# RWKV-6 attention with a SiLU block: level-5 scores in array quarters that serve both batch rows at once, instead of in array eighths

## The chip, the cores and the metric

The kernel runs on one core of one Trainium2 chip. The metric is the device time of a launch in microseconds (us). TensorE (PE) multiplies matrices into PSUM; VectorE (DVE), ScalarE (ACT) and GpSimd (POOL) do elementwise work; SyncE (SP) issues most of the DMA transfers. PEld names TensorE's weight loads, which overlap its matmuls.

## The reference, cut to what matters

First comes a recurrent attention over 768 tokens, for 4 batch rows and 8 heads of 48 channels; then a two-layer network over all 3072 tokens.

```python
for t in range(S):                      # S = 768, state: (B, H, 48, 48)
    cur = einsum('bhd,bhe->bhde', u * k[t], v[t])
    y[t] = einsum('bhd,bhde->bhe', r[t], state + cur)
    state = w[t][..., None] * state + einsum('bhd,bhe->bhde', k[t], v[t])
x = y.transpose(0, 2, 1, 3).reshape(B * S, H * D)     # 3072 x 384
h = x @ w_in                                          # 384 x 2048
out = (h * (1 / (1 + exp(-h)))) @ w_out               # 2048 x 384
```

The decay w multiplies the state per channel, so the weight of key s in the output of token t is the product of all decays between them. Everything is float32.

## The kernel before, in words

**Units.** The tokens are cut into 6 pieces of L = 128. Two batch rows (NB = 2) are worked on together, so there are 12 units, numbered 0 to 11, of 128 tokens by two batch rows. The 8 heads form NP = 4 pairs; the two heads of a pair (index `e`) lie on partitions 0 to 47 and 64 to 111. A row `q` of the tiles `tr` (queries) and `score` is a batch row and a pair, 8 in all.

**Levels.** Inside a unit, the score of query t and key s contains the decays between them. The kernel builds these products by halving. At level l the 128 tokens are cut into blocks of c = 2^l. Queries in an odd block meet the keys of the even block just before it; queries (`tr`) and keys (`tk`) have by then been multiplied with the decays up to the border between the two blocks. Level 6 has one pair of blocks of 64 tokens for a batch row, level 5 has two pairs of blocks of 32. Keys of the second batch row are kept in reversed order of time. That way the even blocks of both batch rows fit side by side in one row of 128 keys, `tk[i][rows, X[l % 2] + p, :]`: where one batch row has no keys to offer, the other has. `corner(l, x)` says which batch row and which query block the x-th stretch of c keys belongs to.

**Scores.** `score_products` (L688) computes one level of a unit on TensorE. In units 1 to 11 it doesn't use the whole array at once, but parts of it: `rows` picks one head of the pair, which is one half of the array's rows, and the stretch of keys picks a part of its columns. In quarters, 64 keys are the stationary matrix (48 x 64) and the moving matrix holds 64 queries. For levels 1 to 4 these are 32 queries of each of the two batch rows, so half of each result belongs to a key of one batch row and a query of the other, and nobody reads it. Level 6 has one batch row for each quarter. Level 5, before the change, is in eighths: 32 keys by 32 queries, one batch row each, four stretches for a pair and head.

**Readers.** In most units (2 to 11) `burst` computes two levels together, 3 with 4 and 5 with 6, into the PSUM tiles `p_sc` and `p_m` (`p_o` in unit 2). `keep_level` copies levels 5 and 6 into `score` with ScalarE (L801), block by block. Unit 1 instead copies under a mask (L722). Unit 0 has another form at L712 for levels 1 to 5, and so has level 4 of unit 2. After the burst, `grow_queries` (L627, DVE) multiplies the queries for the next step in place, and `y_state`, `y_values`, `update` use the scores.

**Order of work.** The order on each engine is written out by hand. From unit 3 on, the attention of unit i is interleaved with the network of units i - 1 and i - 2: `up` (L1001, the first layer, with the SiLU at L1010 on ScalarE), `sums` (L1049, DVE sums of activations for a seven-product scheme of the second layer) and `quarter` (L1067, the second layer, with DVE additions at L1076). `mix` lists the attention's groups, and the loop at L1166 puts network steps between them. `bonus_write` (L604) and `block_write` (L577) put the u-term on the diagonal of `score`. POOL multiplies the keys (`grow_keys`, L645) ahead of each burst. In the first 90 us, the weights are also brought into another form piece by piece (`head_weight`, `tail_weight`, `join_weight`, `add_weight`, L223 to L255).

Of the kernel before, what the change touches and what calls it, by code (L numbers as in the profile page):

```python
# [38 lines left out]
def kernel(  # L39
# [11 lines left out]
    nc = tc.nc  # L51
# [10 lines left out]
    X = 0, NP + Q  # L62
# [275 lines left out]
    for l in range(NL):  # L338
        c, ni = 1 << l, L >> (l + 1)
# [18 lines left out]
    tw, tr, tk, diag, kq, xt = {}, {}, {}, {}, {}, {}  # L358
# [320 lines left out]
    def dims_of(have, start, *dims):  # L679
        return bass.AP(tensor=have.tensor, offset=have.offset + start, ap=[have.ap[0], *dims])  # L680

    def corner(l, x):

        return x % 2, x if x % 2 == 0 else (L >> l) - 1 - x
# [3 lines left out]
    def score_products(i, l, queries, sc):  # L688
        c, ni = 1 << l, L >> (l + 1)
        if (i > 0 or l == NL - 1) and (i, l) != (NTOK, FIRST + 1):  # L690
            for p in range(NP):
                for x in range(4 if c == 32 else 2):
                    for e in range(2):
                        rows = slice(PD * e, PD * e + D)
                        if c >= 32:
                            b, first = corner(l, x)
                            q = (p, 2 * NP - 1 - p)[b]
                            to, have = sc[e][x * c:(x + 1) * c, q, first // 2 * c:(first // 2 + 1) * c], queries[rows, q, (first + 1) * c:(first + 2) * c]
                        else:
                            apart = 2 * (NP - p) - 1  # L700
                            to = dims_of(sc[e][x * 64:(x + 1) * 64, p, :], 32 * x, [apart * L // 2 + 32 - 64 * x, 2], [1, 32])
                            have = dims_of(queries[rows, p, :], 64 * x + c, [apart * L + 64 - 128 * x, 2], [2 * c, 32 // c], [1, c])
                        m = 32 if c == 32 else 64
                        nc.tensor.matmul(to, lhsT=tk[i][rows, X[l % 2] + p, x * m:(x + 1) * m], rhs=have, start=True, stop=True)  # L704
            return

        for p in range(NP):
            for e in range(2):
                rows = slice(PD * e, PD * e + D)

                apart, r_p, s_p = 2 * (NP - p) - 1, queries[rows, p, :], sc[e][:, p, :]
                nc.tensor.matmul(bass.AP(tensor=s_p.tensor, offset=s_p.offset,  # L712
                                         ap=[s_p.ap[0], [apart * L // 2, 2], [1, L // 2]]),
                                 lhsT=tk[i][rows, X[l % 2] + p, :],
                                 rhs=bass.AP(tensor=r_p.tensor, offset=r_p.offset + c,
                                             ap=[r_p.ap[0], [apart * L, 2], [2 * c, ni], [1, c]]),
                                 start=True, stop=True)
# [7 lines left out]
    def scores(i, l, *between):  # L725
        c, ni = 1 << l, L >> (l + 1)

        odd = i == 0 and l % 2 == 1
        sc = [ps.tile([128, Q, L // 2], F32, name="p_h", bufs=2) if odd else bank("p_sc", Q, L // 2) for e in range(2)]
        score_products(i, l, tr[i], sc)  # L730
        if i < NTOK and l + 2 < NL:
            odd_keys(i, l + 1)
# [53 lines left out]
    def burst(i, l):  # L786

        made[i, l] = [bank("p_sc", Q, L // 2) for e in range(2)]
        made[i, l + 1] = [second[0].tile([128, Q, L // 2], F32, name="p_o", bufs=2) if i == NTOK else bank("p_m", Q, L // 2) for e in range(2)]
        score_products(i, l, before.pop((i, l)), made[i, l])  # L790
        score_products(i, l + 1, tr[i], made[i, l + 1])
# [417 lines left out]
```

## Time and profile before

| | |
|---|---|
| median of 3 runs | 600.91 us (600.6, 600.91, 602.53) |
| the profiled execution's own time | 601.18 us |
| its span | 599.4 us |
| busy: PE, PEld | 590.6 us (99%), 529.7 us (88%) |
| busy: DVE, ACT, POOL | 417.5, 232.8, 361.3 us |
| DMA | 53.45 MB, 89 GB/s in the mean |
| matmul records at L704, the line concerned | 1312 into `p_sc`, 608 into `p_m`, 32 into `p_o` |

The span is the time from the first to the last instruction that the profiler recorded; the profiled execution's own time is 1.78 us longer, which lies around the span. A line of the profile names the engine, the source line, the operation and what it writes from what. `x` counts records; a float32 matmul of the program appears as two. Some matmul records can be missing. In square brackets stands how long the engine had been idle before the instruction, and which engine and line released it; "issue" means that it waited for nothing that the profile shows.

### The profile page before, as it was taken

Reading aid. Unit: us, or ns where it says so; the run is one execution under the profiler, and the core shown is the slowest. Engines: PE = TensorE matmul, PEld = TensorE weight load, DVE = VectorE, ACT = ScalarE, POOL = GpSimd, SP = SyncE. Lnnn points to the kernel's source line nnn. Section 1 sums busy time; section 2 is a strip of 40 time slices with the busy share of each in tenths; the row PEclk is TensorE's granted clock in tenths of the full one; section 3 lists DMA queues with packets and bytes.
Section 4 is the critical chain, followed back from the end, with each engine's and each line's share of the span. In section 5 each row is a group of like instructions: output and inputs, shape, how many; then the busy total and the mean of one; then the engine's idle time right before and its main releaser. Section 6 shows DMA issues by size and latency. Waiting matters only on the chain.

```text
span 599.4 us, 15465 instructions
## 1 busy us (share of the span) xinstructions
PE 590.6 (99%) x6142; PEld 529.7 (88%) x6142; DVE 417.5 (70%) x709; ACT 232.8 (39%) x516; POOL 361.3 (60%) x414
## 2 busy tenths in 40 slices
PE   8999999999999999999999999999999999999997
PEld 7787876799899899899899889889889889889997
DVE  7879788798696695696696696687588587542041
ACT  6788884431530530540350351361351251250110
POOL 6998778357678568278578478577567567500000
PEclk9999999999999999999999999999999999999999
DMA  9966794342542543642643643643543531101000
GB/s 225 306 143 176 165 277 49 54 80 48 129 61 62 108 68 54 134 63 52 137 63 54 134 61 53 135 61 53 112 77 52 121 57 27 36 2 28 27 1 26
DMA packets 203080, 53.45 MB, mean 89 GB/s; under 512 B 186752, under 2 KB 194816, under 8 KB 203008
## 3 DMA queue, kind: packets, MB, share of 16 engines
q1 hardware_dynamic: 201424, 51.88, 42.3%
q8 instruction: 48, 0.79, 0.6%
q10 hardware_dynamic: 1584, 0.59, 0.5%
q14 instruction: 24, 0.20, 0.1%
HBM read 43.21 MB, written 5.24 MB: 81 GB/s over the span
## 4 chain that ended last, share of the span: by engine, by line
PE 74%; DVE 9%; POOL 4%; DMA 4%; ACT 3%; issue 3%; SPq 3%; DVEq 0%; POOLq 0%; ACTq 0%
PE p_h L1001 31%; PE p_o L1067 31%; PE p_m L1023 3%; PE p_sc L704 2%; PE p_m L865 2%; DVE temps L1049 2%; SPq L123 1%; PE p_m L844 1%; PE p_m L704 1%; DVE score L722 1%; POOL w_in_sb L255 1%; DMA tokens_w<-in_w_dram 1%; POOL tk L645 1%; DVE p_w L242 1%; DMA raw<-in_r_dram 1%
## 5 line engine op out<-in xcount | busy, mean ns | idle before, releaser
L1001 PE MATMUL p_h<-xt,w_in_sb 128*128 128x256 f32 x1152 | 259.5, 382 | 0.8 <-POOL tk L669 0.7
L1001 PEld LDWEIGHTS p_h<-xt,w_in_sb 128*128 128x128 f32 x1152 | 215.6, 190 | 32.1 <-POOL tk L669 0.9
L1010 ACT ACTIVATE gt<-p_h 128x512 f32<-128x512 f32 x90 | 53.5, 596 | 175.4 <-PE p_h L1001 175.1
L645 POOL TENSOR_TENSOR tk<-tk,tw 128x256 f32<-128x256 f32 x128 | 94.6, 759 | 32.9 <-issue 20.8
L1067 PE MATMUL p_o<-own,temps 128*128 128x192 f32 x528 | 88.7, 327 | 0.7 <-DVE temps L1076 0.7
L1067 PEld LDWEIGHTS p_o<-own,temps 128*128 128x128 f32 x528 | 86.0, 190 | 1.6 <-DVE temps L1076 1.6
L507 POOL TENSOR_TENSOR ruk<-tokens_rk 128x768 f32<-128x768 f32 (+1 forms) x32 | 50.6, 1594 | 60.8 <-DMA tokens_rk<-in_k_dram 36.9
L1067 PE MATMUL p_o<-w_out_sb,gt 128*128 128x192 f32 x508 | 86.6, 327 | 0.0
L1067 PEld LDWEIGHTS p_o<-w_out_sb,gt 128*128 128x128 f32 x508 | 83.3, 190 | 1.0 <-DVE partial L1076 0.4
L1049 DVE TENSOR_TENSOR temps<-gt 128x256 f32<-128x256 f32 x84 | 54.9, 653 | 25.5 <-ACT gt L1010 25.3
L627 DVE TENSOR_TENSOR tr<-tr,tw 128x512 f32<-128x512 f32 x61 | 54.8, 899 | 18.3 <-PE p_m L704 14.6
L422 POOL TENSOR_TENSOR tw<-tw 128x256 f32<-128x256 f32 (+6 forms) x83 | 41.0, 494 | 35.8 <-DVE tw L374 31.9
L615 ACT COPY tk<-tk 128x256 f32<-128x256 f32 x52 | 21.0, 403 | 105.2 <-POOL tk L645 77.6
L1049 DVE TENSOR_TENSOR temps<-temps,gt 128x256 f32<-128x256 f32 x43 | 32.6, 759 | 1.5
L722 DVE COPY_PREDICATED score<-mask,p_sc 128x512 f32<-128x512 int8 x42 | 31.2, 799 | 3.5 <-PE p_sc L704 3.3
L1067 PE MATMUL p_o<-w_out_sb,temps 128*128 128x192 f32 x176 | 30.4, 326 | 0.0
L541 DVE TENSOR_REDUCE block_sums<-ruk 128x4 f32<-128x192 f32 (+1 forms) x48 | 24.2, 546 | 7.1 <-POOL ruk L507 7.1
L1067 PEld LDWEIGHTS p_o<-w_out_sb,temps 128*128 128x128 f32 x176 | 28.9, 190 | 0.0
L1076 DVE TENSOR_TENSOR partial<-p_o,partial 128x192 f32<-128x192 f32 x33 | 11.7, 354 | 24.6 <-PE p_o L1067 24.6
L1076 DVE TENSOR_TENSOR temps<-p_o,partial 128x192 f32<-128x192 f32 x22 | 7.9, 358 | 29.8 <-PE p_o L1067 23.5
L870 ACT COPY yt<-p_m 48x512 f32<-48x512 f32 x40 | 23.2, 580 | 13.8 <-PE p_m L865 13.1
L704 PEld LDWEIGHTS p_sc<-tr,tk 48*32 48x32 f32 (+1 forms) x1312 | 18.2, 119 | 11.1 <-issue 8.1
(188 smaller groups left out, 821.9 us busy)
## 6 DMA issues: line engine op xcount, KB each, us to landing
w_out_sb<-in_moe_w_in_dram SPq DMA_DIRECT2D x6, 768.0 KB, 7.5
w_out_sb<-in_moe_w_out_dram SPq DMA_DIRECT2D x4, 768.0 KB, 5.6
own<-in_moe_w_out_dram SPq DMA_DIRECT2D x4, 768.0 KB, 6.4
tokens_rk<-in_r_dram SPq DMA_DIRECT2D x8, 384.0 KB, 4.5
tokens_rk<-in_k_dram SPq DMA_DIRECT2D x8, 384.0 KB, 5.5
tokens_w<-in_w_dram SPq DMA_DIRECT2D x8, 384.0 KB, 6.6
xt<-yt SPq DMA_DIRECT2D x60, 48.0 KB, 2.0
raw<-in_w_dram SPq DMA_DIRECT2D x80, 32.0 KB, 2.0
```

What stands on the lines that cost most here:

```text
L422: engine.tensor_tensor(out=up, in0=t[:, :, 0::2], in1=t[:, :, 1::2], op=ALU.mult)
L507: mul = lambda out, one, two: nc.gpsimd.tensor_tensor(out=out, in0=one, in1=two, op=ALU.mult)
L541: add = lambda out, have: nc.vector.tensor_reduce(out=out, in_=have, axis=mybir.AxisListType.X, op=ALU.add)
L627: nc.vector.tensor_tensor(out=odd, in0=odd, in1=tw[i][l][:, :, 0::2][:, :, :, None].to_broadcast([128, Q, L >> (l + 1), c]), op=ALU.mult)
L645: nc.gpsimd.tensor_tensor(out=out, in0=have, in1=odd_products(i, l, b, *blocks), op=ALU.mult)
L704: nc.tensor.matmul(to, lhsT=tk[i][rows, X[l % 2] + p, x * m:(x + 1) * m], rhs=have, start=True, stop=True)
L722: nc.vector.copy_predicated(out=dst, mask=masks[l][:, :, None].to_broadcast([128, NB, NP, ni, c]), data=sc[e].rearrange("p (b q) (i c) -> ...
L870: nc.scalar.copy(out=yt[i][PD * e:PD * e + D, x::2, :, :], in_=p_yt[i, e][PD * x:PD * x + D].rearrange("p (q b) t -> p q b t", b=NB))
L1001: nc.tensor.matmul(p_h[:, a, :], lhsT=w_in_sb[:, c, f * 128:(f + 1) * 128], rhs=xt[i][:, c, :], start=(c == 0), stop=(c == KC - 1))
L1010: nc.scalar.activation(out=gt[i, m], in_=p_h, func=AF.Silu)
L1049: nc.vector.tensor_tensor(out=out, in0=one, in1=two, op=op)
L1067: nc.tensor.matmul(p, lhsT=left(f), rhs=right[:, f, :], start=(f == 0), stop=(f == FH - 1))
```

## The change

In `score_products`, level 5 (c = 32) no longer has its own branch. It takes the form of levels 1 to 4: two stretches of 64 keys instead of four of 32, and for each a moving matrix of 64 queries, 32 from each of the two batch rows. The special form with `corner` stays for level 6 (c = 64) alone. Level 5 of a unit is then 16 matmuls of 48 x 64 by 64, where it was 32 of 48 x 32 by 32. The results that are needed land at the same places of PSUM, and every reader is unchanged; as much again of the tile, which level 5 left unwritten, now gets products that nobody reads.

```diff
         if (i > 0 or l == NL - 1) and (i, l) != (NTOK, FIRST + 1):
             for p in range(NP):
-                for x in range(4 if c == 32 else 2):
+                for x in range(2):
                     for e in range(2):
                         rows = slice(PD * e, PD * e + D)
-                        if c >= 32:
+                        if c == 64:
                             b, first = corner(l, x)
                             q = (p, 2 * NP - 1 - p)[b]
                             to, have = sc[e][x * c:(x + 1) * c, q, first // 2 * c:(first // 2 + 1) * c], queries[rows, q, (first + 1) * c:(first + 2) * c]
                         else:
                             apart = 2 * (NP - p) - 1
                             to = dims_of(sc[e][x * 64:(x + 1) * 64, p, :], 32 * x, [apart * L // 2 + 32 - 64 * x, 2], [1, 32])
                             have = dims_of(queries[rows, p, :], 64 * x + c, [apart * L + 64 - 128 * x, 2], [2 * c, 32 // c], [1, c])
-                        m = 32 if c == 32 else 64
-                        nc.tensor.matmul(to, lhsT=tk[i][rows, X[l % 2] + p, x * m:(x + 1) * m], rhs=have, start=True, stop=True)
+                        nc.tensor.matmul(to, lhsT=tk[i][rows, X[l % 2] + p, x * 64:(x + 1) * 64], rhs=have, start=True, stop=True)
```

## The prediction

> **What bounds the kernel now.** I read the page's busy times first, then busy time by stage, then TensorE's own waits, then single bursts of level 5.
>
> ```profile
> PE 590.6 (99%) x6142; PEld 529.7 (88%) x6142; DVE 417.5 (70%) x709; ACT 232.8 (39%) x516; POOL 361.3 (60%) x414
> ```
>
> TensorE (PE) sets the time, but 99% is a mean. By stage (columns: span, then busy time of PE, weight loads, DVE, ACT, POOL):
>
> ```profile
> 88.90:180.40 91.50, 91.03 (x1040) 76.67 (x1040) 76.40 (x115) 35.23 (x84) 57.72 (x63) 1.00 0.44 72
> 180.40:273.10 92.70, 92.49 (x993) 84.72 (x993) 68.80 (x113) 30.67 (x76) 61.95 (x70) 1.00 0.44 80
> 273.10:557.20 284.10, 284.10 (x2945) 262.17 (x2946) 189.88 (x330) 89.82 (x223) 169.15 (x191) 1.00 0.37 69
> ```
>
> From 273 us on PE has no idle time. Before that it has a few short waits. PE's instructions in order of time, only those with a wait (bracket: idle before, and who ended it):
>
> ```profile
> 88.91 0.70 PE L704 MATMUL p_sc<-tr,tk 48*64 48x64 f32 x32 [0.39 <-POOL tk L669]
> ...
> 132.36 2.87 PE L1067 MATMUL p_o<-own,temps 128*128 128x192 f32 x16 [0.19 <-DVE temps L1076]
> ...
> 180.44 5.47 PE L1067 MATMUL p_o<-own,temps 128*128 128x192 f32 x32 [0.31 <-DVE temps L1076]
> ...
> 273.07 5.47 PE L1067 MATMUL p_o<-own,temps 128*128 128x192 f32 x32 [0.17 <-DVE temps L1076]
> ```
>
> These four places decide the forecast. PE time saved after 273 us reaches the end; time saved before one of them reaches it only if the releaser moves too.
>
> Now the operation itself, in unit 6: weight loads in order of time, levels 3 and 4 (quarters, 48x64) and then levels 5 (eighths, 48x32) and 6 (quarters).
>
> ```profile
> 283.85 0.56 PEld L704 LDWEIGHTS p_sc<-tr,tk 48*64 48x64 f32 x32 [0.23 <-issue]
> 284.31 0.56 PEld L704 LDWEIGHTS p_m<-tr,tk 48*64 48x64 f32 x32
> 284.94 12.82 PEld L1001 LDWEIGHTS p_h<-xt,w_in_sb 128*128 128x128 f32 x60
> ...
> 298.09 0.65 PEld L704 LDWEIGHTS p_sc<-tr,tk 48*32 48x32 f32 x64 [0.33 <-issue]
> 298.77 0.56 PEld L704 LDWEIGHTS p_m<-tr,tk 48*64 48x64 f32 x32
> 299.40 5.04 PEld L1001 LDWEIGHTS p_h<-xt,w_in_sb 128*128 128x128 f32 x24
> ```
>
> Each float32 matmul of the program is two records, so level 5 is 64 and level 3 is 32. From start to start of the next group, level 3 takes 0.46 us (284.31 - 283.85) and level 5 takes 0.68 (298.77 - 298.09). Level 4 (284.31 to 284.94) and level 6 (298.77 to 299.40) both take 0.63, so level 6 pays nothing for what stands before it. The same 0.46 to 0.47 and 0.68 to 0.69 stand in the bursts at 144, 191, 237 and 330 us, and at 113, 205, 344 and 527 us.
>
> **What the Trainium skill says.** "TensorEngine Tiling (Array Packing)", Performance Considerations, Instruction Overhead: a matmul has a floor of some 60 cycles, so one gains nothing from a dimension that is already small. That fits: level 5's 64 records load in 0.65 us, 10 ns each, and level 3's 32, with twice the columns, in 0.56 with the last load's own 0.13: 14 ns each. Halving the columns doesn't halve the record. The same page, Overview, Key Properties, says that a change of tiling mode drains the array. The trace agrees in size: from level 5's last load (298.09 + 0.65 - 0.105 = 298.64) to level 6's first is 0.13 us, between levels 3 and 4 it is 0.03. So 0.22 is about 0.12 of issue and 0.10 of change of mode. "GPSIMD Engine Reference", Key points, says that GpSimd (POOL) shares its SBUF interfaces with VectorE; in this trace the sums of L1049 take 0.42 us, and about 1 us each while POOL multiplies at 254 to 258 us. That matters below for unit 5.
>
> **The change part by part.** Level 5 in the per-corner form is used in units 1 to 11 (unit 0 takes the full-height form at L712). It loses 32 matmuls (64 records) and gains 16 (32 records) in each: 176 matmuls fewer. The instructions of DVE, ACT, POOL and SP, their order and their waits are the same; no DMA is moved. The new records have level 3's shape (48x64 weights, 64 moving columns as two blocks) and its place ahead of a second quarter group, so I take 0.46. That is 0.68 - 0.46 = 0.22 us of PE per unit, 11 x 0.22 = 2.4 us of PE work. Half of each product is not used, but the copies at L801 take the same rows and columns as before and unit 1's masked write reads the same bank, so readers cost the same.
>
> One wait moves: the third matmul of a group waited for POOL's second key product (batch row 1); now the first waits for both. Nothing else was to run in between. In unit 2 the last key product ends at 111.5 us for a burst at 113.13, in unit 6 at 292.7 for 298.09: cost nothing.
>
> Results come earlier by less than 0.22. PE's two level-5 forms, from first start to last end:
>
> ```profile
> 283.85 0.69 PE L704 MATMUL p_sc<-tr,tk 48*64 48x64 f32 x32
> ...
> 298.09 0.76 PE L704 MATMUL p_sc<-tr,tk 48*32 48x32 f32 x64
> ```
>
> Level 5's scores are ready 0.07 sooner (0.76 - 0.69), and only level 6 and what follows moves by the whole 0.22. So it matters which of the two a later wait hangs on. DVE and ACT at units 2, 3 and 5:
>
> ```profile
> 116.87 2.52 DVE L604 COPY_PREDICATED score<-own_mask,both_b 128x1024 f32<-128x1024 int8 x2 [1.57 <-ACT score L801]
> 162.57 0.42 DVE L1049 TENSOR_TENSOR temps<-gt 128x256 f32<-128x256 f32 x1 [2.74 <-ACT gt L1010]
> 252.94 0.69 DVE L627 TENSOR_TENSOR tr<-tr,tw 128x512 f32<-128x512 f32 x1 [0.56 <-PE p_m L704]
> ```
>
> ```profile
> 113.91 2.14 ACT L801 COPY score<-p_sc 32x128 f32<-32x128 f32 x8 [2.28 <-PE p_sc L704]
> 158.17 2.25 ACT L801 COPY score<-p_sc 32x128 f32<-32x128 f32 x8 [0.68 <-DVE score L604]
> ```
>
> Unit 1 (59.42 us): PE next waits for POOL's weight pieces (0.2 us of weight load idle at 63.69, then 88.91). Gain 0; at most 0.13.
>
> Unit 2 (113.13): DVE is busy without a gap from 116.87 to the release at 132.3. Its start hangs on ACT's copies, and those on level 5's end: it moves by 0.07. PE arrives 0.22 sooner and waits 0.15 longer. Gain 0.07.
>
> Unit 3 (155.97): ACT's copies wait for DVE's L604, not for PE, and DVE from 162.57 follows ACT without a gap to the release at 180.4. Nothing moves, and the wait at 180.44 grows from 0.31 to 0.53. Gain 0. Unit 2's 0.07 passes, since that DVE work comes, by the chain that ended last, from PE at 144.4.
>
> Unit 4 (205.46): PE runs without a wait to the next burst. Gain 0.22.
>
> Unit 5 (251.46): DVE's 20 busy us before the wait at 273.07 start when level 6 is done (0.56 idle <-PE). DVE's earlier work ends at 252.38, so it can start 0.22 + 0.22 + 0.07 = 0.51 sooner and still be the waiting side. Work shared with POOL on either side of that shift is the same in sum. Gain 0.22.
>
> Units 6 to 11: no PE wait follows. The release that is late at 273.07 ends at 317.73 in unit 6, where PE needs it at about 319.4: 1.6 us of slack. Gain 6 x 0.22 = 1.32.
>
> Sum: 0.07 + 0.22 + 0.22 + 1.32 = 1.83 us. The profiled execution took 601.18 us, span 599.4 and 1.78 around it; it becomes 599.35, span 597.6. The median of the runs, 600.91, is 0.27 lower and becomes 599.1. A measurement here can tell about 0.3% (1.8 us) from no change; the forecast stands at that border.
>
> **The rivals.** *Other engines take part of it* (chance 0.27): in unit 5 DVE and POOL fall on each other so that DVE doesn't gain (0.22 lost), or another 0.5 us of slack goes, as where one DVE sum lands behind a POOL product (0.42 becomes about 1.2). For: those slow sums at 254 us. Against: 1.6 us of slack from unit 6 on. Gain 0.8 to 1.5: 599.4 to 600.1.
>
> *All 2.4 arrives* (0.15): the short waits before 273 us depend on when DMA and POOL fall, and an execution without them keeps everything: 598.5.
>
> *Slower through the first wait* (0.05): if POOL's second key product came after PE, each burst would stand for it, about 0.6 us (a pair of them takes 1.19), so 11 x (0.6 - 0.22) = 4.2: 605. It decides from the point where POOL's slack, now 1.6 us in unit 2 and over 5 in unit 6, falls under 0; against it, every steady burst's idle time is "issue", not POOL.
>
> That the change does nothing is no case: PE's stream is shorter by 176 matmuls. That quarters are bound by streaming and so slower than eighths is answered by level 3: 0.46 for the same columns.
>
> **How the numbers follow.** My forecast has 0.53, with a spread of about 0.6 us around 599.1 from the runs' own scatter (600.6 to 602.53). Half of it is beyond 0.3%; with the 0.15 of the full gain and a little of the first rival, faster is 0.45. Same is 0.49: the other half and most of the first rival. Slower is 0.06: the third, and scatter. The range goes from 598.3 (full gain, a little scatter) to 600.6 (a gain of 0.8 with the upper scatter); outside is about 0.15.
>
> **What would show it.** In the changed profile: level 5 as 32 records of 48x64, 0.46 from its first load to level 6's; level 6 still 0.63; a burst period of 45.78 us from unit 6 on, now 46.00 (283.85 to 329.85); PE's wait at about 180 us near 0.53 and at 132 near 0.34; the wait near 272.5 still about 0.17. I am wrong if level 5 takes over 0.5, if a POOL wait stands before it, or if new PE waits appear after 273.

## The result, and the profile after

| | before | after |
|---|---|---|
| median of 22 runs each | 601.24 us (600.6 to 602.76) | 599.37 us (598.71 to 602.5) |
| ratio | | 0.9971, 95% interval 0.9964 to 0.9978 |
| profiled execution, its span | 601.18, 599.4 us | 599.81, 598.0 us |
| matmul records | 6142 | 5790 |

The changed kernel is faster by 0.29%, some 1.7 us, and the interval of the ratio stays below 1. The forecast was 599.1 us, with a gain of 1.83. A line number of the changed kernel is one less than before from L703 on.

The first lines of the page after:

```profile
span 598.0 us, 14761 instructions
...
PE 588.5 (98%) x5790; PEld 528.1 (88%) x5790; DVE 418.0 (70%) x709; ACT 233.1 (39%) x516; POOL 363.3 (61%) x414
```

There are 352 records fewer, 176 matmuls by two, and 2.1 us less of PE busy time. Level 5 and level 6 of unit 6, weight loads in order of time:

```profile
298.06 0.56 PEld L703 LDWEIGHTS p_sc<-tr,tk 48*64 48x64 f32 x32 [0.33 <-issue]
298.52 0.56 PEld L703 LDWEIGHTS p_m<-tr,tk 48*64 48x64 f32 x32
299.16 0.94 PEld L1000 LDWEIGHTS p_h<-xt,w_in_sb 128*128 128x128 f32 x5
```

Level 5 takes 298.52 - 298.06 = 0.46 us, it was 0.68; level 6 takes 0.64, it was 0.63. The period of a unit, from the same answer over the whole span (starts of level 3 in units 6 and 7):

```profile
283.82 0.56 PEld L703 LDWEIGHTS p_sc<-tr,tk 48*64 48x64 f32 x32 [0.23 <-issue]
...
329.61 0.56 PEld L703 LDWEIGHTS p_sc<-tr,tk 48*64 48x64 f32 x32 [0.23 <-issue]
```

That is 45.79 us, 46.00 before. PE's instructions with a wait, from 88 us on:

```profile
88.95 0.70 PE L703 MATMUL p_sc<-tr,tk 48*64 48x64 f32 x32 [0.40 <-POOL tk L669]
...
132.36 2.87 PE L1066 MATMUL p_o<-own,temps 128*128 128x192 f32 x16 [0.37 <-DVE temps L1075]
...
179.93 5.47 PE L1066 MATMUL p_o<-own,temps 128*128 128x192 f32 x32 [0.17 <-DVE temps L1075]
...
273.04 5.47 PE L1066 MATMUL p_o<-own,temps 128*128 128x192 f32 x32 [1.10 <-DVE temps L1075]
```

The same four places wait, and none is new. But the wait near 273 us grew from 0.17 to 1.10 us, and PE goes on at 273.04, where it went on at 273.07 before. So in this execution nothing that was saved before 273 us arrived. What arrived came after: from there to the end of the span are 598.0 - 273.04 = 324.96 us, and 599.4 - 273.07 = 326.33 before, 1.37 us less, six bursts of 0.22 to 0.23. This execution took 599.81 us, 0.44 more than the median of the 22 runs, so it needn't show all that the median kept.

What made PE wait is on DVE, in unit 5. DVE after, in order of time:

```profile
250.57 2.52 DVE L577 COPY_PREDICATED score<-spare 128x1024 f32<-128x1024 int8 x2
252.97 0.69 DVE L627 TENSOR_TENSOR tr<-tr,tw 128x512 f32<-128x512 f32 x1
```

Before, L577 began at 249.87, and L627 then waited 0.56 us for PE's level 6. Now L577 begins 0.70 us later and L627 follows it without a wait for PE, at 252.97, where it had begun at 252.94. PE had come to its burst 0.73 us sooner (250.73 for 251.46), and DVE didn't follow. L577 writes what comes back from a transfer through DRAM (`block_move`: `kept` out, `spare` in). SyncE's queue after:

```profile
230.50 6.29 SPq L928 DMA_DIRECT2D xt<-yt  x10
236.83 5.21 SPq L123 DMA_DIRECT2D raw<-in_r_dram  x8
242.14 0.40 SPq L1079 DMA_DIRECT2D out_dram<-ob  x1
242.64 0.38 SPq L1079 DMA_DIRECT2D out_dram<-temps  x1
243.11 0.39 SPq L560 DMA_DIRECT2D kept<-block_sums  x1
```

One transfer is issued straight after the other. DVE's sums for `kept` were done at 240.25, and it was issued 2.9 us later, when the queue came to it; before, they were done at 240.97 and it was issued at 242.93. What this explains of the 1.10 us, and what it doesn't, comes out of the second execution below.

### The profile page after: what moved, and what is told of

Its sections match the earlier page's. It is cut to its first block, busy times and chain, and to the rows that moved or that the text cites. A ratio compares the mean times of both kernels' runs of the same rounds, so it can differ in the third digit from the quotient of the medians.

```text
span 598.0 us, 14761 instructions
## 1 busy us (share of the span) xinstructions
PE 588.5 (98%) x5790; PEld 528.1 (88%) x5790; DVE 418.0 (70%) x709; ACT 233.1 (39%) x516; POOL 363.3 (61%) x414
## 4 chain that ended last, share of the span: by engine, by line
PE 77%; DVE 5%; DMA 5%; SPq 5%; POOL 3%; ACT 2%; issue 2%; DVEq 0%; POOLq 0%; ACTq 0%
PE p_h L1000 33%; PE p_o L1066 31%; SPq L123 3%; PE p_m L1022 3%; PE p_sc L703 2%; PE p_m L864 2%; PE p_m L843 2%; PE p_m L703 1%; DMA raw<-in_r_dram 1%; DMA tokens_rk<-in_k_dram 1%; DVE score L721 1%; DMA tokens_w<-in_w_dram 1%; POOL w_out_sb L255 1%; PE p_sc L819 1%; POOL tk L645 1%
## 5 line engine op out<-in xcount | busy, mean ns | idle before, releaser
L645 POOL TENSOR_TENSOR tk<-tk,tw 128x256 f32<-128x256 f32 x128 | 93.6, 752 | 33.6 <-issue 20.7
L507 POOL TENSOR_TENSOR ruk<-tokens_rk 128x768 f32<-128x768 f32 (+1 forms) x32 | 53.8, 1691 | 57.2 <-DMA tokens_rk<-in_k_dram 37.2
L1048 DVE TENSOR_TENSOR temps<-gt 128x256 f32<-128x256 f32 x84 | 53.2, 633 | 25.6 <-ACT gt L1009 25.3
L627 DVE TENSOR_TENSOR tr<-tr,tw 128x512 f32<-128x512 f32 x61 | 57.5, 942 | 16.0 <-PE p_m L703 12.5
L654 POOL TENSOR_TENSOR tk<-tk,tw 128x256 f32<-128x256 f32 x32 | 27.6, 883 | 0.0
```

The source lines that it names most:

```text
L507: mul = lambda out, one, two: nc.gpsimd.tensor_tensor(out=out, in0=one, in1=two, op=ALU.mult)
L627: nc.vector.tensor_tensor(out=odd, in0=odd, in1=tw[i][l][:, :, 0::2][:, :, :, None].to_broadcast([128, Q, L >> (l + 1), c]), op=ALU.mult)
L645: nc.gpsimd.tensor_tensor(out=out, in0=have, in1=odd_products(i, l, b, *blocks), op=ALU.mult)
L654: nc.gpsimd.tensor_tensor(out=have, in0=have, in1=odd_products(i, l, b, [2, NP * ni]), op=ALU.mult)
L1048: nc.vector.tensor_tensor(out=out, in0=one, in1=two, op=op)
```

## Experiments

**Where the gain comes from.** Two kernels have the change in a part of the units.

```diff
-                for x in range(4 if c == 32 else 2):
+                for x in range(4 if c == 32 and i < 6 else 2):
...
-                        if c >= 32:
+                        if c == 64 or c == 32 and i < 6:
...
-                        m = 32 if c == 32 else 64
+                        m = 32 if c == 32 and i < 6 else 64
```

This is `steady`; `early` has `i > 5` in the three places.

> Quarters for level 5 in units 6 to 11 only; units 1 to 5 keep the eighths. Theory: each burst saves 0.22 us of TensorE, and after 273 us nothing stands in its way, so all six arrive: 6 x 0.22 = 1.32 us less than before, ratio 0.9978, burst period 45.78 us from unit 6 on. Rival (the gain comes from the early units, or from how transfers happen to fall): well under 1 us. TensorE's wait for DVE near 273 us is as before, 0.2 us and more.

> Quarters for level 5 in units 1 to 5 only. By the prediction's sum these give 0.07 + 0.22 + 0.22 = 0.51 us, ratio 0.9992. Rival, from the profile of the changed kernel: the release at 273 us follows SyncE's queue, which is full from about 199 to 243 us, and not TensorE; then TensorE's wait near 273 us grows by what was saved ahead of it and the gain is near 0 in such an execution, ratio 0.9995 to 1.0005.

Measured: `steady` 600.07 us for 601.6 before, ratio 0.9974 (0.9961 to 0.9988); `early` 601.2 us, ratio 0.9991 (0.9982 to 1.0). Both agree with the forecast's parts, 0.9978 and 0.9992. The interval of `early` reaches from 1.1 us to nothing, so it doesn't tell 0.51 from 0. PE's wait near 273 us in `steady` is 0.11, where 0.2 and more was expected.

The traces say more than the times. I cut each span at three places where PE's weight loads start again after DVE's release and at the start of unit 2's level 5. All in us:

| kernel, level 5 in units 2 to 5 / 6 to 11 | unit 2's level 5 to 132 | 132 to 180 | 180 to 273 | 273 to end |
|---|---|---|---|---|
| before, eighths / eighths | 19.23 | 48.07 | 92.63 | 326.34 |
| steady, eighths / quarters | 19.23 | 47.53 | 92.56 | 325.01 |
| early, quarters / eighths | 19.17 | 48.12 | 92.77 | 326.34 |
| after, quarters / quarters | 19.18 | 47.57 | 93.11 | 324.96 |
| after, second execution | 19.19 | 47.59 | 92.37 | 324.99 |

The last column falls by 1.33 to 1.38 exactly where units 6 to 11 have quarters. The first falls by 0.04 to 0.06 where unit 2 has them, 0.07 in the forecast. The second changes by 0.5, but not with the change: `steady` has eighths there and is as short as after, `early` has quarters and is as long as before. It goes with SyncE's queue. In unit 3 DVE's L604 waits for what ScalarE copies of four small transfers, `diag<-own_sums`. SyncE before, and then after:

```profile
151.58 0.38 SPq L1080 DMA_DIRECT2D out_dram<-temps  x1
152.04 2.45 SPq L467 DMA_DIRECT2D diag<-own_sums  x4
```

```profile
149.83 0.38 SPq L1079 DMA_DIRECT2D out_dram<-temps  x1
151.53 2.45 SPq L467 DMA_DIRECT2D diag<-own_sums  x4
```

Before, they stand straight behind another transfer; after, the queue was free when they were ready. From their issue to the end of the stage there are 28.4 us in all five executions.

In the third stage quarters should have taken off 0.44; the three executions with quarters have a mean of 92.75, the two with eighths 92.60. No gain is seen there, but the three differ by 0.74 among themselves, so they can't exclude one. What lies ahead of the table, 113.13 us before, varies more: 113.97 in `steady`, 114.50 in `early`, 113.18 and 113.76 after. The profiled execution of `early` took 602.66 us and was the slowest of its 14 runs.

**A second execution of the changed kernel.**

> A second look at the changed kernel. Level 5 0.46 us in every burst, the period 45.78 from unit 6 on. If the time of the release near 273 us follows SyncE's queue, its distance from TensorE's arrival differs from the first look's 1.10 us and moves with the time at which kept is issued in unit 5 (243.1 there); if it follows TensorE as in the prediction, the wait is 0.2 here and the first look is an exception.

Measured: 599.67 us. PE's wait, SyncE's transfers and ScalarE's copies of what came back:

```profile
272.91 5.47 PE L1066 MATMUL p_o<-own,temps 128*128 128x192 f32 x32 [0.35 <-DVE temps L1075]
```

```profile
243.43 0.40 SPq L560 DMA_DIRECT2D kept<-block_sums  x1
246.22 1.00 SPq L563 DMA_DIRECT2D spare<-kept  x2
249.16 1.00 ACT L570 COPY spare<-spare 32x64 f32<-32x64 f32 x4 [0.44 <-DMA spare<-kept]
```

The same two in the first execution:

```profile
245.71 1.00 SPq L563 DMA_DIRECT2D spare<-kept  x2
249.27 1.00 ACT L570 COPY spare<-spare 32x64 f32<-32x64 f32 x4 [1.04 <-DMA spare<-kept]
```

The wait is 0.35 here and not 1.10. `kept` was issued 0.3 later than in the first execution, and yet the release came 0.1 sooner. The reason is that in the first execution the second of the two transfers `spare<-kept` took 3.1 us to land, and at most 2.5 in the other four. So some 0.6 of the 1.10 is this one slow landing, and nothing ties it to the change. Apart from it the release does follow the queue: PE restarts 26.7 us after the issue of `spare<-kept` here and in `early`, 27.3 after it in the first execution.

What stays is DVE's stretch: from L627 to the restart of PE's weight loads there are 20.05 us here (252.86 to 272.91), 20.07 in the first execution, 20.07 in `early`, 20.12 before and 20.06 in `steady`. L627 begins at the later of two events, the end of L577 and the end of level 6. With eighths it was level 6 that came last (L627 waited 0.56 us for PE before, 0.41 in `steady`). In all three with quarters it was L577: PE had come to level 5 sooner, and the queue had not. `spare<-kept` was issued 5.0 to 5.2 us ahead of PE's level 5 with quarters, 5.7 with eighths (251.46 - 245.74 before). The change took PE out of the place of the last one.

**SyncE's queue as the cause.** In unit 5 the loads for a later unit are put behind `kept`, once with eighths and once with quarters.

```diff
-        behind = groups[10 if i < NPAIR else 5 if i == NPAIR else 2:][:4 if i + NSLOT >= len(units) else None]
+        behind = groups[10 if i < NPAIR else 5 if i in (NPAIR, NPAIR + 1) else 2:][:4 if i + NSLOT >= len(units) else None]
```

> Level 5 in eighths as before, but in unit 5 the eight loads of raw in_r that stand on SyncE's queue ahead of the transfer of block_sums to kept come after it. If SyncE's queue is what makes DVE late at 273 us: kept is issued about 1.7 us sooner (near 241 instead of 242.9), ScalarE's copies of spare and DVE's L577 come 2 us or more sooner, and TensorE's wait near 273 us is gone: 0.2 us and up to 1 us faster than before, ratio 0.9985 to 0.9997. If DVE's own work sets it, the wait stays and the time is that of before.

> The changed kernel with the same order of transfers in unit 5. If SyncE's queue took the early units' gain, all of the prediction's sum arrives against eighths_kept_first: 0.07 + 0.22 + 0.22 + 1.32 = 1.83 us, and no wait of TensorE near 273 us; against before 2.0 to 2.8 us, ratio 0.9953 to 0.9966. If not, it stays at the changed kernel's 0.9971.

Measured: eighths 601.45 us, ratio 1.0003 (0.999 to 1.0016); quarters 600.66 us, ratio 0.9978 (0.9967 to 0.999). Neither median reaches its forecast, and against `eighths_kept_first` the quarters gain 0.79 us by the medians where 1.83 was expected. With eighths, SyncE, DVE and POOL in unit 5:

```profile
241.66 0.33 SPq L560 DMA_DIRECT2D kept<-block_sums  x1
```

```profile
249.71 4.14 DVE L577 COPY_PREDICATED score<-spare 128x1024 f32<-128x1024 int8 x2
254.21 1.82 DVE L627 TENSOR_TENSOR tr<-tr,tw 128x512 f32<-128x512 f32 x1 [0.37 <-PE p_m L704]
```

```profile
250.86 1.81 POOL L507 TENSOR_TENSOR ruk<-tokens_rk 128x768 f32<-128x768 f32 x1 [3.56 <-DMA tokens_rk<-in_k_dram]
```

The same line of POOL before:

```profile
253.87 1.81 POOL L507 TENSOR_TENSOR ruk<-tokens_rk 128x768 f32<-128x768 f32 x1 [7.85 <-DMA tokens_rk<-in_k_dram]
```

`kept` goes out 1.3 us sooner, and PE's wait near 273 us is gone in both kernels. L577 begins only 0.16 us sooner than before by the clock, not the 2 expected. With eighths the wait isn't gone because DVE starts sooner: L627 waits for PE as before, and begins 1.47 us after the start of level 5, 1.48 before. What is shorter is DVE's stretch after it. `tokens_rk` stands behind `kept` in the queue and moved with it, so POOL's four products of L507 begin 3 us sooner and are done at 258.05, not at 259.93. DVE's eight sums of L1049 next to L627 take 4.5 us for 7.8 before: the slow ones beside POOL, up to 2.03 us, are fewer, and the others take 0.41 to 0.43. So the edit moved two things at once.

With quarters the same line of DVE shows what the earlier `kept` did:

```profile
253.47 2.28 DVE L627 TENSOR_TENSOR tr<-tr,tw 128x512 f32<-128x512 f32 x1 [1.79 <-PE p_m L703]
```

L627 waits for PE again, 1.79 us, and not for L577. PE's waits, with quarters:

```profile
180.65 5.47 PE L1066 MATMUL p_o<-own,temps 128*128 128x192 f32 x32 [0.19 <-DVE temps L1075]
...
239.96 12.32 PE L1000 MATMUL p_h<-xt,w_in_sb 128*128 128x256 f32 x56 [0.53 <-DMA xt<-yt]
286.14 12.32 PE L1000 MATMUL p_h<-xt,w_in_sb 128*128 128x256 f32 x56 [0.16 <-DMA xt<-yt]
319.98 5.47 PE L1066 MATMUL p_o<-own,temps 128*128 128x192 f32 x32 [0.37 <-DVE temps L1075]
```

In these executions other waits took the place of that one. PE waits 0.53 us (0.38 with eighths) for `xt<-yt`, which is on the same queue. It is issued ahead of the place of the edit, so this wait isn't the edit's doing; `early`, where the order is untouched, has it too, 0.22 at 240.81. The loads put back fall into unit 6, and with quarters PE waits there as well. So two things are shown: SyncE's backlog is what made L577, and with it DVE, later than PE in the kernels with quarters, and with `kept` sooner PE comes last again. Not shown is that the place of `kept` alone ends the wait near 273 us, since POOL's products moved too; nor that the queue would otherwise have let the early gain through. A kernel in which SyncE issues fewer transfers in units 4 and 5 wasn't tried.

**What 0.22 consists of.** Two kernels with other shapes. In `wide_keys`, level 5 has quarters' weights with eighths' queries:

```diff
-                            to, have = sc[e][x * c:(x + 1) * c, q, first // 2 * c:(first // 2 + 1) * c], queries[rows, q, (first + 1) * c:(first + 2) * c]
+                            part = slice(x // 2 * 64, x // 2 * 64 + 64) if c == 32 else slice(x * c, (x + 1) * c)
+                            to, have = sc[e][part, q, first // 2 * c:(first // 2 + 1) * c], queries[rows, q, (first + 1) * c:(first + 2) * c]
...
-                        m = 32 if c == 32 else 64
-                        nc.tensor.matmul(to, lhsT=tk[i][rows, X[l % 2] + p, x * m:(x + 1) * m], rhs=have, start=True, stop=True)
+                        if c < 32:
+                            part = slice(x * 64, (x + 1) * 64)
+                        nc.tensor.matmul(to, lhsT=tk[i][rows, X[l % 2] + p, part], rhs=have, start=True, stop=True)
```

> Level 5 with 64 keys as in quarters, but 32 queries of one batch row as in eighths: 32 matmuls, 64 records of 48x64 weights and 32 moving columns in units 1 to 11. What sets the spacing of records? If the weight columns (64 take 14 ns, as in levels 3 and 4): level 5 takes 64 x 14 = 0.90 us from its first load to level 6's. If the moving columns or a floor for each record (8.7 ns in the eighths): 64 x 8.7 = 0.56, and with no change of tile size ahead of level 6 about 0.58. Every later group is as before, 0.63 for level 6.

In `six_eighths`, level 6 too has 32 keys:

```diff
-                for x in range(4 if c == 32 else 2):
+                for x in range(4 if c >= 32 else 2):
...
-                            b, first = corner(l, x)
+                            b, first = corner(l, x * 32 // c)
...
-                            to, have = sc[e][x * c:(x + 1) * c, q, first // 2 * c:(first // 2 + 1) * c], queries[rows, q, (first + 1) * c:(first + 2) * c]
+                            to, have = sc[e][x * 32:(x + 1) * 32, q, first // 2 * c:(first // 2 + 1) * c], queries[rows, q, (first + 1) * c:(first + 2) * c]
...
-                        m = 32 if c == 32 else 64
+                        m = 32 if c >= 32 else 64
```

> Level 5 in eighths as before, and level 6 also with 32 keys (48x32 weights, 64 queries, 64 records), so that the tile size doesn't change between them. If 0.10 us of level 5's 0.68 is the change of tile size, level 5 takes 0.58 to level 6's first load; if there is no such cost, 0.68. Level 6: if moving columns set the spacing, 64 x 14 = 0.9 us and more; if weight columns or a floor for each record do, about 0.56 and the exit of 0.17, so 0.73, against 0.63 before.

Weight loads of unit 6, first `wide_keys`, then `six_eighths`:

```profile
299.81 1.04 PEld L706 LDWEIGHTS p_sc<-tr,tk 48*64 48x64 f32 x64 [0.33 <-issue]
300.74 0.58 PEld L706 LDWEIGHTS p_m<-tr,tk 48*64 48x64 f32 x32
301.39 0.30 PEld L1003 LDWEIGHTS p_h<-xt,w_in_sb 128*128 128x128 f32 x2
```

```profile
301.57 0.65 PEld L704 LDWEIGHTS p_sc<-tr,tk 48*32 48x32 f32 x64 [0.33 <-issue]
302.15 0.72 PEld L704 LDWEIGHTS p_m<-tr,tk 48*32 48x32 f32 x64
302.96 1.59 PEld L1001 LDWEIGHTS p_h<-xt,w_in_sb 128*128 128x128 f32 x8
```

`six_eighths` shows the change of tile size: level 5 takes 302.15 - 301.57 = 0.58 with level 6 in the same tile size, 0.68 with another. So 0.10 of the 0.22 was the change of size and 0.12 the records.

What makes the records of the eighths dear is less clear. In `wide_keys` level 5 takes 0.93 us (300.74 - 299.81), twice the quarters' 0.46, for the same number of records as the eighths and the same 32 queries: (1.04 - 0.13) / 63 = 14.4 ns from record to record, where the eighths have (0.65 - 0.105) / 63 = 8.7. So one floor for every record, whatever its shape, doesn't explain both. Level 6 of `six_eighths`, with 32 weight columns and 64 queries, has (0.72 - 0.105) / 63 = 9.8 ns, and takes 0.81 to the next group, not the 0.73 expected. This looks as if the columns of the weights set the spacing, but two things speak against taking it for shown. First, `wide_keys` changed more than the weights' columns. Its stretches follow each other in pairs on the same part of the array, so fewer parts can work side by side, and 32 queries there may take as long as 64 spread over all four. Nor do the queries count for nothing in general. In unit 5 before, `y_state` multiplies 48 weight columns by 128 moving ones, and its records start (1.13 - 0.27) / 31 = 28 ns apart, 0.27 being the time of one:

```profile
258.78 1.13 PE L844 MATMUL p_m<-tr,state 48*48 48x128 f32 x32
```

Second, 8.7 ns is a mean and no spacing. Level 5 of unit 6 before, taken in two windows:

```profile
298.09 0.24 PEld L704 LDWEIGHTS p_sc<-tr,tk 48*32 48x32 f32 x33 [0.33 <-issue]
298.33 0.40 PEld L704 LDWEIGHTS p_sc<-tr,tk 48*32 48x32 f32 x31
```

The first 33 records start some 4 ns apart, the last at 298.23. Then no load starts for about 0.1 us, and the other 31 follow at some 10 ns. All eleven bursts of the kernel before do this, and level 5 of `six_eighths` as well. A level in quarters has only 32 records and ends before that point. The stop is nearly as large as the 0.12 us to be explained; what causes it no run shows.

One execution of each took 604.49 and 605.11 us, beside 601.55 of the kernel before. Single executions of the kernel before lie between 600.75 and 604.96 us, so these times prove little. For `wide_keys`, 11 x (0.93 - 0.68) = 2.75 would come near the 2.94. For `six_eighths`, two levels in 0.58 + 0.81 instead of 1.31 make only 0.9 of 3.56; part of the rest is in waits, 1.33 us of it one for `xt<-yt` at 243 us.

## Why the prediction was right

**The term 0.22 per burst** held to the hundredth, and the wait for both key products cost nothing: every steady level 5 is idle before it for "issue", 0.33 us, as before.

**Units 6 to 11, 1.32 us.** Right: 1.33 to 1.38 in each of the three executions that have quarters there and the old order of transfers, and no PE wait after 273 us. This is the greater part of the result.

**Units 1 and 2, 0 and 0.07.** Right. After unit 1, PE's first wait for POOL past 88 us ends at 88.95, 88.91 before. For unit 2 it was 0.04 to 0.06 in the stage up to 132 us, and the wait there grew to 0.37 us (0.34 was named). That results are ready only 0.07 sooner, while the following group moves by 0.22, was the right thing to look for.

**Unit 3, 0.** The stage shows no gain that goes with the change. But the named wait near 180 us, 0.53, was wrong: it is 0.17 and 0.19 in the two executions of the changed kernel. The prediction followed ScalarE's copies back to L604 and stopped there. L604 hangs on `diag<-own_sums`, and so the release moves by 0.5 us with the queue; the wait of one profile was no fixed number to add to.

**Units 4 and 5, 0.44.** This step failed in the executions that were profiled. It said that DVE's earlier work ends at 252.38, so that DVE "can start 0.22 + 0.22 + 0.07 = 0.51 sooner and still be the waiting side". It took the end of L577 for a fixed time with 0.56 us of room. L577 hangs on a transfer whose issue stands in SyncE's full queue, and it ended 0.6 to 0.7 later in both executions after. Then L577 and not PE released DVE, and PE waited for it: 1.10 and 0.35 us, where 0.17 was named; some 0.6 of the 1.10 was one slow landing. The prediction also read DVE's sums beside POOL at 254 to 258 us as "about 1 us each"; they take 1.23 to 2.03 us there, and `eighths_kept_first` shows DVE's stretch 2.2 us shorter when POOL's products come sooner.

**The sum.** By the stages, 1.33 + 0.05 = 1.4 us go with the change in every profiled execution. The measured gain is 1.7 with an interval of about 1.3 to 2.2. So the forecast of 1.83 holds, but with a term for units 4 and 5 that the profiled executions don't show; whether other executions deliver a part of it is left open, since `early` allows anything from 0 to 1.1 us. If they don't, the sum came out near the median by luck. The first rival, in which other engines take part of the early gain, describes what was seen in the traces, though with SyncE's queue in place of POOL; its gain of 0.8 to 1.5 us is too small for the median. The prediction put the border between the same and faster at 0.3%, with 0.49 and 0.45 on the two sides. At 0.29% the side was a matter of chance.

**The reason for eighths being slow.** The prediction quoted from the Trainium skill's page "TensorEngine Tiling (Array Packing)", Performance Considerations, Instruction Overhead, a floor for each matmul, and found that it fits. That isn't shown. Records with 32 queries follow at 8.7 ns in the eighths and 14.4 in `wide_keys`, so no single floor fits both, and the eighths' own records start at 4 ns, stop, and go on at 10. What served the forecast was not the reason but the price: 0.46 us, read off level 3, which has the shape wanted. The change of tiling mode as a cost (the same page, Tiling Modes, Key Properties) was right, with 0.10 us.

## What to carry to other kernels

Time saved on the bounding engine counts in full only after the last place where it waits for another. Before such a place, look for every event that the releaser could have started on, and take the room to the second latest one as a range over executions, above all where it comes through a full transfer queue. When small tiles share the array, more and smaller matmuls can take longer for the same result: here 64 records of eighths took 0.58 us and 32 of quarters 0.46. Price a new shape by a group in the same trace that has it already, and keep neighbouring groups in one tile size. When a wait differs between two executions, follow it back to the single transfer before blaming the change.

## What was not expected of the hardware

With 48-row float32 tiles working side by side in the array, 64 weight loads of 32 columns didn't follow evenly: 33 started some 4 ns apart, then came a stop of about 0.1 us, and the rest followed at some 10 ns. Loads of 64 columns, 32 in a group, followed at 14 ns. Going from 32-column to 64-column tiles cost 0.10 us. And SyncE, which counts no busy time on the page, issued transfers nearly back to back from about 199 to 243 us, most of them at 0.4 to 0.7 us each: for `kept` in unit 5 its place in the queue, and not the readiness of the data, decided when it left, 2.0 us after its data before and 2.9 after the change.
